# Attention and gated products on one core: down products split in two, summary scores for 128 queries at a time, a new order

## The chip, the core and the metric

The kernel runs on one core of a Trainium2 chip. The core has a matrix engine (TensorE, PE in the profile; its weight loads are a track of their own, PEld), VectorE (DVE), ScalarE (ACT), GpSimd (POOL) and SyncE (SP), which here issues all transfers. Time is the device time of one execution in microseconds (us), the median over several runs. All times of this section and the next ones are of the kernel before.

## The reference, cut to what is computed

```python
k_sum = k.reshape(B, H, nb, 32, D).max(axis=3)          # B 4, H 8, S 768, D 64, nb 24
v_sum = v.reshape(B, H, nb, 32, D).mean(axis=3)
scores_l = q @ k.T / 8, kept where |i - j| < 16, else -1e9
scores_s = q @ k_sum.T / 8 + log(32)
a = softmax(concat(scores_l, scores_s))                 # 768 + 24 columns
x = (a @ concat(v, v_sum)) as rows of 512               # 3072 tokens
h = x @ w_in                                            # 512 -> 2048
out = (h * cos(h)) @ w_out                              # 2048 -> 512
```

Each query sees the 31 keys around it and 24 block summaries of its sequence. The two large products at the end hold nearly all of the arithmetic.

## The kernel before, in words

The 3072 tokens are cut into 8 blocks of 384, two to a sequence. A block has 4 groups (a, b, c, d in the order's names), each a pair of heads. For a group the kernel lays q and k out with the head dimension on the partitions, the first head on partitions 0 to 63 and the second on 64 to 127 (`qd`, `kd`), where the last 24 columns of `kd` are the summaries of k. A group's 384 queries are six tiles of 64 (`t`); tile `t` belongs to chunk `c = t // 2` and half `s = t % 2`, and its scores stand in a bank of PSUM per head, in partitions `s * 64` and up, columns 0 to 95 for a window of 96 keys and columns 96 to 119 for the 24 summaries. `scores` (L562) issues for each tile and head one product with 96 columns and one with 24, all with a 64 by 64 block of q as weights: 24 products for a group. They are in full float32, so each becomes two pairs of a weight load and a matmul in the trace: 48. For the groups of the first two blocks the mask is added by products with a 128 by 128 identity as weights and 360 columns (L549). Then come maximum, exponent, sums, the turning of the probabilities (in the first three blocks by products with the identity, L619: 120 columns of weights) and `values` (L663: 12 products with 120 by 64 weights), which leave x split into a high and a low part (`xh`, `xl`).

The gated part runs in 128 steps (8 blocks by 16 slices of the hidden dimension). A step has `up` (L707: 12 products, 384 columns), then on ACT and DVE `turns`, `residue`, `sine`, `square`, `gate`, then `high_part` (`gh`, a rounded copy, on ACT or DVE) and `low_part` (`gl`, the rest, on POOL or DVE), then `down` (L751: for each of three chunks of 128 tokens the products gh by the high weights, gh by the low weights, gl by the high weights, 512 columns each, added in one bank per chunk). After the last step of a run `take` copies the three sums, negated, to a buffer and `store` sends them out. The 16 slices of the weights are split into high and low parts by ScalarE, VectorE and GpSimd in the first third of the span.

The order of everything is written out by hand: a long string `ORDER` of tokens (`d2.sc.3.4` is scores of group d of block 2 into banks 3 and 4, `s39.up.0` is the up products of step 39 into bank 0, a last `a`, `v` or `p` names ScalarE, VectorE or GpSimd). The tokens are issued in this order and each engine executes its own instructions in it; the SP queue too issues its transfers in it and waits in it.

Of the kernel before, what the change touches and what calls it, by code (L numbers as in the profile page):

```python
# [10 lines left out]
F32 = mybir.dt.float32  # L11
F32R = mybir.dt.float32r
# [15 lines left out]
c0.q b0.k a0.q a0.k d0.k c0.k b0.tk.0.0 v0_0.l b0.tk.1.1 b0.ck.0.a b0.ks.0 a0.tq.2 b0.ck.1.a b0.ks.1 v0_1.l a0.cq.a  # L28
a0.tk.0.3 a0.tk.1.4 a0.ck.0.a a0.ks.0 b0.q a0.ms.5.6 a0.ck.1.a a0.ks.1 d0.tk.0.7 d0.tk.1.0 w1.l d0.ck.0.a d0.ks.0
a0.sc d0.ck.1.a d0.ks.1 c0.tk.0.1 a0.z.1.a c0.tk.1.2 c0.ks.0 c0.tq.3 a0.z.0.a d0.q c0.ms.4.7 c0.ks.1 c0.ck.0.a a0.mx  # L30
c0.ck.1.a c0.cq.a v0_0.h.v a0.su w0.l c0.sc v0_1.h.v v0_0.s.p a0.ex c0.v b0.tq.0 b0.ms.6.5 v0_1.s.v b0.cq.a c0.z.1.a
b0.sc c0.z.0.a a0.sm a0.v w1.ab.0 c0.mx d0.tq.1 b0.z.0.a d0.ms.2.3 a0.iv w1.cl a0.nm b0.z.1.a d0.cq.a w1.sh.6.7 a0.m
d0.sc c0.su w1.lb a0.tp.0.0 w0.ab.1 a0.tp.1.4 d1.q w1.fb.0 a0.cp.0.a w2.l a0.cp.1.a w0.cl d0.z.1.a w1.hi.a w5.l
w0.sh.0.1 a0.va.5 d0.z.0.a b0.m w1.lo.p w0.lb c0.ex d0.m a0.xh.a d0.mx c0.sm d0.su w3.l c0.iv w2.ab.1 a0.xl c0.nm
w0.fb.0 d0.ex b0.v c0.tp.0.6 w2.cl w0.hi.a d0.sm c0.tp.1.7 c0.cp.0.a w0.lo.p c0.m w2.sh.2.3 c0.cp.1.a w2.lb w5.ab.1
c1.q w2.fb.0 a1.q d0.iv w2.hi.a w5.cl d0.nm d0.v w5.sh.4.5 c0.va.0 w4.l w5.lb w3.ab.1 w2.lo.p d1.m d0.tp.0.1 c0.xh.a
b0.mx d0.tp.1.6 c0.xl d0.cp.0.a b0.su a1.tq.7 b1.q w5.fb.0 d0.cp.1.a d0.va.2 a1.cq.a a1.m b0.ex w3.cl a1.ms.3.0
w5.hi.a w3.sh.6.7 d1.v a1.sc d0.xh.a w5.lo.p b0.sm w4.ab.1 c1.tq.1 c1.v c1.ms.4.5 w3.lb a1.z.1.a a1.z.0.a b1.tq.0
b0.iv b1.m w4.cl b0.nm c1.cq.a b1.cq.a a1.mx c1.sc c1.m w4.sh.0.1 c1.z.1.a a1.su b0.tp.0.3 c1.z.0.a b0.tp.1.5 d0.xl
a1.v b0.cp.0.a w4.lb b1.ms.4.2 b0.cp.1.a a1.ex w8.l c1.mx b0.va.3 b1.v a1.sm b1.sc c1.su b0.xh.a b0.xl d1.tq.5  # L40
b1.z.1.a a1.iv s0.up.3 a2.q w4.fb.0 a1.nm c1.ex b1.z.0.a b2.v c1.sm w4.hi.a d1.ms.2.0 c1.iv w3.fb.1 s0.tu c1.nm
d1.cq.a a1.tp.0.1 w7.l w4.lo.v s1.up.4 w3.hi.a w9.l a1.cp.0.a w3.lo.p b1.mx w8.ab.0 w6.l d1.sc s0.re s1.tu w8.cl
a1.tp.1.5 v1_0.l s2.up.6 d1.z.0.a w10.l b1.su d1.z.1.a s1.re a1.cp.1.a s0.si d1.mx a1.va.7 w8.sh.0.1 d1.su a2.tq.2
a2.v c1.tp.0.5 s0.sq w8.lb s1.si s1.sq c1.cp.0.a s0.ga s1.ga c1.tp.1.5 s0.hi.a w8.fb.1 s1.hi.a s0.lo.p c1.cp.1.a
w9.ab.0 s0.dn.3.4.5 s1.lo.p w8.hi.v b2.q s2.tu d1.ex s2.re w8.lo.p a2.cq.v a1.xh.v s3.up.0 a1.xl s2.si d1.sm v1_0.s.p
d1.iv w9.cl c1.va.1 s2.sq d1.nm v1_1.l s3.tu s1.dn c1.xh.a s3.re w7.ab.1 c1.xl s2.ga s2.hi.a w7.cl s4.up.2 s3.si
s2.lo.p w9.sh.6.7 s3.sq b1.ex v1_1.s.p s3.ga d1.tp.0.1 w9.lb d1.tp.1.0 s2.dn s4.tu b1.sm v1_2.l d1.cp.1.a d1.cp.0.a
s4.re s5.up.0 s3.hi.a b1.iv w9.fb.0 b1.nm s4.si w9.hi.v s3.lo.p d1.va.1 w7.sh.6.7 s4.sq d1.xh.a w9.lo.p s3.dn s5.tu
w7.lb w10.ab.1 s5.re s4.ga s5.si v1_2.s.p d1.xl s4.hi.a b1.tp.0.2 w7.fb.0 s5.sq b1.tp.1.1 b1.cp.0.a b1.cp.1.a s4.lo.p
s5.ga w12.l w7.hi.a b1.va.2 s5.hi.v v1_3.l s4.dn w10.cl s5.lo.p b1.xh.a b1.xl w7.lo.p w10.sh.6.7 s6.up.1 w6.ab.1  # L50
w10.lb w10.fb.0 s7.up.0 s6.tu v1_3.s.p s6.re w10.hi.a w6.cl s5.dn s7.tu s6.si w10.lo.p v1_4.l s6.sq b2.m s7.re s8.up.2
s5.ta.0.a s6.ga s5.ta.1.v s6.hi.a s5.st.0 s5.ta.2.a w6.sh.6.7 s5.st.1 s6.lo.p w12.ab.0 s5.st.2 a2.m w6.lb v1_4.s.p
s6.dn.1.3.4 s8.tu s7.si s8.re s7.sq w12.cl s8.si v1_5.l s9.up.5 s8.sq s7.ga s8.ga s7.hi.a w6.fb.1 s8.hi.a s7.lo.p
s7.dn s9.tu s8.lo.p w12.sh.6.7 w11.l w6.hi.a s9.re w6.lo.p w12.lb s9.si s10.up.0 s9.sq s9.ga w12.fb.0 s9.hi.a s8.dn
s10.tu s9.lo.p s10.re w12.hi.a w15.l v1_5.s.v w11.ab.1 w12.lo.p s11.up.2 v1_6.l s10.si w11.cl s10.sq s9.dn s11.tu
s11.re s10.ga s11.si w11.sh.6.7 s10.hi.a s12.up.5 s11.sq s10.lo.p w15.ab.0 w11.lb v1_6.s.p s10.dn s12.tu s11.ga s12.re
s11.hi.a w11.fb.1 s12.si s11.lo.p v1_7.l s13.up.0 s12.sq s12.ga w11.hi.a w13.l w15.cl s12.hi.a w15.sh.6.7 s11.dn
s13.tu s12.lo.p s13.re w11.lo.p w15.lb s13.si s12.dn s13.sq s13.ga w15.fb.0 s13.hi.a s13.lo.p s14.up.2 w13.ab.1
w15.hi.v w13.cl w15.lo.p s13.dn s14.tu v1_7.s.v s14.re a2.k s15.up.5 w13.sh.6.7 s14.si s14.sq s14.ga w13.lb s14.hi.a
s16.up.0 s15.tu s14.lo.p s15.re w13.fb.0 s15.si s14.dn s15.sq s16.tu s15.ga w14.l w13.hi.a s16.re a2.tk.0.2 s15.hi.a  # L60
w13.lo.p a2.tk.1.6 a2.ks.0 a2.ck.0.a s17.up.7 b2.k a2.ck.1.a a2.ks.1 s16.si s16.sq s15.lo.p a2.sc.5.2 s16.ga s16.hi.a
s15.dn s17.tu a2.z.1.v s16.lo.p s17.re w14.ab.1 a2.z.0.v a2.mx s17.si s16.dn s17.sq w14.cl a2.su s17.ga s17.hi.a
w14.sh.6.7 b2.tk.0.0 s18.up.2 b2.ck.0.a s17.lo.p a2.ex w14.lb s17.dn w14.fb.0 s18.tu a2.sm w14.hi.a b2.tk.1.5 s18.re
b2.tq.6 w14.lo.p b2.ck.1.a c2.k s19.up.7 b2.ks.1 s18.si b2.ks.0 c2.q b2.cq.v a2.iv b2.sc.5.0 a2.nm s18.sq s19.tu
s18.ga s20.up.6 s19.re s18.hi.a b2.z.0.v s19.si s18.lo.p b2.z.1.v s19.sq b2.mx a2.tp.0.2 s20.tu a2.tp.1.5 c2.tq.0
a2.cp.0.a s19.ga b2.su s18.dn d2.q c2.cq.v a2.cp.1.a s19.hi.a s20.re b2.ex s19.lo.p c2.tk.0.7 c2.tk.1.2 c2.ks.0 s19.dn
d2.k c2.ks.1 c2.ck.0.a b2.sm c2.ck.1.a s20.si b2.iv s21.up.5 b2.nm s20.sq s20.ga s22.up.0 s21.tu s20.hi.a s21.re
s20.lo.p s21.si s21.sq d2.tk.0.7 s20.dn s22.tu s21.ga d2.ck.0.a d2.ks.0 s21.hi.a s22.re s21.lo.p s22.si a2.va.2 s22.sq
d2.tk.1.6 s22.ga a2.xh.a c2.m s23.up.5 s22.hi.v d2.ck.1.a d2.ks.1 s22.lo.p a2.xl c2.v b2.tp.0.7 s23.tu b2.tp.1.0
c2.sc.6.2 b2.cp.0.a s23.re v2_0.l b2.cp.1.a d2.tq.7 s23.si c2.z.1.v s21.dn a3.q c2.z.0.v s23.sq d2.cq.a c2.mx s23.ga  # L70
c2.su s22.dn.0.2.6 s21.ta.1.1.a s23.hi.v s21.ta.2.0.a s21.st.1 c2.ex s21.st.2 s23.lo.p s24.up.7 c2.sm s25.up.5
s21.ta.0.1.a c2.iv c2.nm s24.tu s21.st.0 s24.re s24.si d2.sc.3.4 s23.dn d2.z.0.v d2.z.1.v s25.tu s24.sq d2.mx s26.up.1
s25.re d2.su s24.ga s25.si a3.qt s24.hi.a s25.sq b3.q s24.lo.p b2.va.3 d2.ex s25.ga s24.dn s25.hi.v b2.xh.v s25.lo.p
# [103 lines left out]
def tile_kernel(  # L177
# [25 lines left out]
    P = 128  # L203
# [491 lines left out]
    class Step:  # L695
# [76 lines left out]
        def take(self, i, *args):  # L772
            *where, eng = args
            if where:
                self.place(i, *where)
            else:
                self.o[i] = late[5][:, i * DM : (i + 1) * DM]
# [134 lines left out]
```

## Time and profile before

| what | value |
|---|---|
| median of 3 runs | 678.67 us (677.88 to 681.73) |
| the profiled execution | 679.78 us, span 678.0 us |
| mean granted TensorE clock | 0.984 |
| PE busy | 641.4 us, 95% |
| PEld busy | 564.8 us, 83% |
| DVE, ACT, POOL busy | 391.1, 411.6, 295.4 us |

The profiled execution took 1.1 us more than the median. In rows of the trace a line gives start and length in us, engine, source line, operation, output and inputs, partitions and columns of the weights (`64*64`), shape of the output and the count of instructions that the row merges. A merged row runs from the first start to the last end. The start of a matmul is recorded and its end is modelled, so rates are read from starts.

### The profile page before, as it was taken

To read this page: it belongs to the slowest core of one execution; us is meant where nothing else is said; L and a number is where in the kernel's file an instruction comes from. 1 tells how busy PE (TensorE), PEld (TensorE's weight loads), DVE (VectorE), ACT (ScalarE), POOL (GpSimd) and SP (SyncE) were. 2 spreads that over 40 slices of the span, in tenths; PEclk is the share of its full clock that TensorE was granted. 3 is DMA by queue.
4 is the path that set the end of the run, shared out by engine and by line. 5 is a ranking of instruction groups with operands and counts; after the bars stand their busy time and mean duration, and the time that the engine had idled before them with its cause. 6 is when DMAs were issued, how large, how long until landed. Compare 5 with 4: busy or idle time off the path is not lost.

```text
span 678.0 us, 13401 instructions
## 1 busy us (share of the span) xinstructions
PE 641.4 (95%) x5180; PEld 564.8 (83%) x5180; DVE 391.1 (58%) x642; ACT 411.6 (61%) x720; POOL 295.4 (44%) x312
## 2 busy tenths in 40 slices
PE   6439989999999999999999999999999999999996
PEld 4327768888888888888898888898898889899895
DVE  3889799987553467426775764248484652232221
ACT  3557887758765467646765765447666565455443
POOL 3665778655432355333444554414353442122221
PEclk9959999999999999999999999999999999999999
DMA  9797924442322323434545453433253440001001
GB/s 221 212 252 195 321 83 159 149 110 59 87 51 54 88 78 112 117 89 95 111 123 129 118 166 95 94 53 89 75 148 90 107 124 29 23 0 47 1 0 47
DMA packets 158543, 71.17 MB, mean 105 GB/s; under 512 B 129552, under 2 KB 147344, under 8 KB 158480
## 3 DMA queue, kind: packets, MB, share of 16 engines
q1 hardware_dynamic: 158480, 70.32, 39.0%
q8 instruction: 41, 0.67, 0.4%
q14 instruction: 22, 0.18, 0.1%
HBM read 52.99 MB, written 14.94 MB: 100 GB/s over the span
## 4 chain that ended last, share of the span: by engine, by line
PE 86%; DMA 5%; DVE 3%; ACT 2%; SPq 2%; POOL 2%; issue 1%; POOLq 0%; ACTq 0%; DVEq 0%
PE banks L707 38%; PE banks L751 37%; PE banks L562 4%; DMA late<-in_moe_w_out_dram 4%; PE banks L663 4%; SPq L449 1%; PE banks L549 1%; PE banks L619 1%; POOL w L349 1%; DMA kn<-in_v_dram 1%; DVE banks L400 1%; DVE banks L392 1%; DVE stage L386 1%; PE banks L495 0%; PE banks L508 0%
## 5 line engine op out<-in xcount | busy, mean ns | idle before, releaser
L707 PE MATMUL banks<-xh,w 128*128 128x384 f32 x1024 | 281.9, 338 | 0.0
L751 PE MATMUL banks<-w,gh 128*128 128x512 f32 x768 | 242.6, 397 | 0.0
L349 POOL TENSOR_TENSOR gl<-t,gh 128x384 fp32r<-128x384 f32 x123 | 126.0, 1026 | 251.1 <-ACT gh L343 185.7
L707 PEld LDWEIGHTS banks<-xh,w 128*128 128x128 f32 x1024 | 186.9, 188 | 4.7 <-DVE xl L349 0.2
L707 PE MATMUL banks<-xl,w 128*128 128x384 f32 x512 | 171.8, 336 | 0.0
L751 PEld LDWEIGHTS banks<-w,gh 128*128 128x128 f32 x768 | 140.2, 188 | 25.6 <-ACT gh L343 0.2
L751 PE MATMUL banks<-w,gl 128*128 128x512 f32 x384 | 151.7, 395 | 0.6 <-POOL gl L349 0.4
L720 DVE SCALAR_TENSOR_TENSOR t<-t,banks 128x384 f32<-128x384 int32 x128 | 70.3, 549 | 127.6 <-ACT t L717 127.4
L717 ACT ACTIVATE t<-banks 128x384 int32<-128x384 f32 x128 | 62.4, 487 | 104.0 <-PE banks L707 100.3
L732 DVE SCALAR_TENSOR_TENSOR t<-t,banks 128x384 f32<-128x384 f32 x128 | 70.2, 549 | 75.5 <-ACT t L728 75.0
L707 PEld LDWEIGHTS banks<-xl,w 128*128 128x128 f32 x512 | 96.1, 188 | 3.8
L725 ACT ACTIVATE t<-t 128x384 f32<-128x384 f32 x128 | 67.2, 525 | 44.1 <-DVE t L720 43.8
L343 ACT CAST gh<-t 128x384 fp32r<-128x384 f32 x115 | 58.8, 512 | 55.1 <-DVE t L732 50.9
L751 PEld LDWEIGHTS banks<-w,gl 128*128 128x128 f32 x384 | 72.0, 188 | 18.0 <-POOL gl L349 2.4
L728 ACT ACTIVATE t<-t 128x384 f32<-128x384 f32 x128 | 67.2, 525 | 3.6
L586 POOL TENSOR_TENSOR sc<-sc,m 128x720 f32<-128x720 f32 x28 | 40.7, 1453 | 41.8 <-DVE m L581 39.0
L610 POOL TENSOR_TENSOR sc<-sc,r 128x720 f32<-128x720 f32 x28 | 38.9, 1392 | 38.5 <-DVE r L607 33.7
L349 POOL TENSOR_TENSOR w<-stage,w 128x1024 fp32r<-128x1024 f32 x15 | 36.6, 2440 | 18.2 <-ACT w L343 17.5
L562 PEld LDWEIGHTS banks<-kd,qd 64*64 64x64 f32 x1344 | 27.5, 132 | 7.9 <-issue 5.5
L602 DVE TENSOR_REDUCE r<-sc 128x6 f32<-128x726 f32 x28 | 25.2, 902 | 14.5 <-ACT sc L599 14.4
L725 ACT ACT_TABLE_LOAD x24 | 30.8, 1283 | 0.4
L562 PE MATMUL banks<-kd,qd 64*64 64x96 f32 (+1 forms) x1344 | 30.4, 231 | 0.1
(97 smaller groups left out, 577.4 us busy)
## 6 DMA issues: line engine op xcount, KB each, us to landing
late<-in_moe_w_in_dram SPq DMA_DIRECT2D x16, 512.0 KB
late<-in_moe_w_out_dram SPq DMA_DIRECT2D x16, 512.0 KB
pd<-stage SPq DMA_DIRECT2D x20, 384.0 KB
vn<-in_v_dram SPq DMA_DIRECT2D x52, 120.0 KB
out_dram<-stage SPq DMA_DIRECT2D x24, 256.0 KB
pt<-pd SPq DMA_DIRECT2D x60, 96.0 KB
kn<-in_v_dram SPq DMA_DIRECT2D x24, 192.0 KB
qn<-in_q_dram SPq DMA_DIRECT2D x80, 48.0 KB
```

The source lines that it names most:

```text
L343: eng.copy(out=out, in_=in_)
L349: eng.tensor_tensor(out=lo, in0=src, in1=hi.bitcast(F32), op=ALU.subtract)
L562: nc.tensor.matmul(out=self.sp[hh][s * QT : (s + 1) * QT, c, lo : lo + n], lhsT=self.qd[rows, t * QT : (t + 1) * QT], rhs=self.kd[rows, ke ...
L586: nc.gpsimd.tensor_tensor(out=self.sc, in0=self.sc, in1=self.m.unsqueeze(2).broadcast_to([P, U, NK]), op=ALU.subtract)
L610: nc.gpsimd.tensor_tensor(out=self.sc, in0=self.sc, in1=self.r.unsqueeze(2).broadcast_to([P, U, NK]), op=ALU.mult)
L707: nc.tensor.matmul(out=self.h, lhsT=w_of(name, self.f)[:, c * P : (c + 1) * P], rhs=x_of(self.blk, part, c), start=n == 0, stop=n == last,)
L717: nc.scalar.activation(out=self.t.bitcast(I32), in_=self.h, func=AF.Copy, scale=1.0 / TWO_PI)
L720: nc.vector.scalar_tensor_tensor(out=self.t, in0=self.t.bitcast(I32), scalar=-TWO_PI, in1=self.h, op0=ALU.mult, op1=ALU.add)
L725: nc.scalar.activation(out=self.t, in_=self.t, func=AF.Sin, scale=0.5)
L728: nc.scalar.activation(out=self.t, in_=self.t, func=AF.Square, scale=math.sqrt(2.0))
L732: nc.vector.scalar_tensor_tensor(out=self.t, in0=self.t, scalar=-1.0, in1=self.h, op0=ALU.add, op1=ALU.mult)
L751: nc.tensor.matmul(out=self.acc[i], lhsT=g[:, i * P : (i + 1) * P], rhs=w_of(name, self.f), start=self.first and n == 0, stop=self.last an ...
```

## The change

It has four parts.

The products of `down` come in two operations. `dh` issues the six products with gh, `dl` the three with gl; in between the order may place other work. In the last step of all, `dh` leaves out the third chunk and `dl` makes up for it.

In `scores` the windows' products stay as they are (64 queries, 96 columns, four of them for a chunk: two halves by two heads), while the summaries' products are made for the 128 queries of a chunk at once: weights of 64 partitions by 128 columns, 24 columns of output over all 128 partitions. A group has 12 products of 96 columns and 6 of 24 columns, instead of 12 and 12.

The last sums of a run that don't go to one of the two stage buffers get a place of their own, in the room of an x part that is no longer needed.

`ORDER` is written anew. In it 38 rather than 13 of the 128 copies `gh` go to VectorE, and 35 rather than 5 of the rests `gl`, the others staying on ScalarE and GpSimd; some of the smaller copies of the attention part move to VectorE as well.

```diff
@@ scores
-            for t in range(U):
-                c, s = divmod(t, 2)
-                k0 = self.base + t * QT
+            for c in range(QC):
+                for s, hh in itertools.product(range(2), range(2)):
+                    rows, k0 = slice(hh * D, (hh + 1) * D), self.base + (2 * c + s) * QT
+                    nc.tensor.matmul(
+                        out=self.sp[hh][s * QT : (s + 1) * QT, c, :W],
+                        lhsT=self.qd[rows, (2 * c + s) * QT : (2 * c + s + 1) * QT], rhs=self.kd[rows, k0 : k0 + W],
+                        start=not self.masks, stop=not self.masks,
+                    )
                 for hh in range(2):
                     rows = slice(hh * D, (hh + 1) * D)
-                    for lo, n, key in ((0, W, k0), (W, NB, KW)):
-                        nc.tensor.matmul(
-                            out=self.sp[hh][s * QT : (s + 1) * QT, c, lo : lo + n],
-                            lhsT=self.qd[rows, t * QT : (t + 1) * QT], rhs=self.kd[rows, key : key + n],
-                            start=not self.masks, stop=not self.masks or (c == QC - 1 and lo == W),
-                        )
+                    nc.tensor.matmul(
+                        out=self.sp[hh][:, c, W:NK],
+                        lhsT=self.qd[rows, c * P : (c + 1) * P], rhs=self.kd[rows, KW : KW + NB],
+                        start=not self.masks, stop=not self.masks or c == QC - 1,
+                    )
@@ down
-            gh, gl = self.gh, self.gl
-            for i in range(NTT):
-                for n, (g, name) in enumerate(((gh, "wo_h"), (gh, "wo_l"), (gl, "wo_h"))):
-                    nc.tensor.matmul(
-                        out=self.acc[i], lhsT=g[:, i * P : (i + 1) * P], rhs=w_of(name, self.f),
-                        start=self.first and n == 0, stop=self.last and n == 2,
-                    )
+            self.products(self.early())
+
+        def early(self):
+            chunks = range(NTT - 1 if self.g == len(steps) - 1 else NTT)
+            return [(i, n) for i in chunks for n in range(2)]
+
+        def down_low(self):
+            early = self.early()
+            rest = [(i, n) for n in range(3) for i in range(NTT) if (i, n) not in early]
+            self.products(sorted(rest) if len(rest) > NTT else rest)
+
+        def products(self, which):
+            for i, n in which:
+                g, name = (self.gl if n == 2 else self.gh), ("wo_h", "wo_l", "wo_h")[n]
+                nc.tensor.matmul(
+                    out=self.acc[i], lhsT=g[:, i * P : (i + 1) * P], rhs=w_of(name, self.f),
+                    start=self.first and n == 0, stop=self.last and n == 2,
+                )
@@ take
-            else:
+            elif self.kind == "first":
                 self.o[i] = late[5][:, i * DM : (i + 1) * DM]
+            else:
+                t = xp.tile([P, 2, TB], F32R, name="last", tag="xh0%d" % (self.blk % 2))
+                self.o[i] = t.rearrange("p c n -> p (c n)")[:, :DM].bitcast(F32)
@@ names
-            lo="low_part", dn="down", fe="fetch", ad="add", ta="take", st="store",
+            lo="low_part", dh="down", dl="down_low", fe="fetch", ad="add", ta="take", st="store",
@@ ORDER, its last tokens
...
+s127.sq s126.dh s127.ga s126.hi.a s126.dl s127.hi.a s127.lo.v s127.dh s127.dl s127.ta.1.1.v s127.ta.0.0.a s127.ta.2.a s127.st.0
+s127.st.2 s127.st.1
```

The first place is on PE: the scores of group d of block 2 and what stands around them, before. Line L562 is `scores`, L707 `up`, L751 `down`; `kd` is the laid-out k, `qd` the laid-out q.

```order
L707 MATMUL banks<-xl_0_506,w_1017 128x384
L707 MATMUL banks<-xh_0_500,w_1017 128x384
L562 MATMUL banks<-kd_102,qd 64x96
L562 MATMUL banks<-kd_102,qd 64x24
...
L751 MATMUL banks<-w_1078,gh 128x512 x2
L751 MATMUL banks<-w_1078,gl 128x512
```

The same group in the change, where L569 is the windows' and L576 the summaries' product, L777 the down products and L721 `up`:

```order
L777 MATMUL banks<-w_1224,gl 128x512 x3
L569 MATMUL banks<-kd_102,qd 64x96 x4
L576 MATMUL banks<-kd_102,qd 128x24 x2
L569 MATMUL banks<-kd_102,qd 64x96 x4
L576 MATMUL banks<-kd_102,qd 128x24 x2
L569 MATMUL banks<-kd_102,qd 64x96 x4
L576 MATMUL banks<-kd_102,qd 128x24 x2
L721 MATMUL banks<-xh_0_434,w_982 128x384
```

Before, products of 64 rows by 96 and by 24 columns alternate 12 times; in the change four windows' products are followed by two of the wide summaries' products, three times. All 32 groups have this form.

The second place is the end of PE's program, before: the down products of the last step.

```order
L751 MATMUL banks<-w_1456,gh 128x512 x2
L751 MATMUL banks<-w_1456,gl 128x512
L751 MATMUL banks<-w_1456,gh 128x512 x2
L751 MATMUL banks<-w_1456,gl 128x512
L751 MATMUL banks<-w_1456,gh 128x512 x2
L751 MATMUL banks<-w_1456,gl 128x512
```

And in the change, the last two steps:

```order
L777 MATMUL banks<-w_1610,gh 128x512 x6
L777 MATMUL banks<-w_1610,gl 128x512 x3
L777 MATMUL banks<-w_1419,gh 128x512 x4
L777 MATMUL banks<-w_1419,gl 128x512 x2
L777 MATMUL banks<-w_1419,gh 128x512 x2
L777 MATMUL banks<-w_1419,gl 128x512
```

The first product with gl stood third in a step; now it stands seventh, and in the last step fifth.

The third place is the end of the SP queue, where the last sums leave, before:

```order
L788 DMA out_dram<-stage_6481 128x512
L788 DMA out_dram<-stage_6483 128x512
L788 DMA out_dram<-stage_6518 128x512
L788 DMA out_dram<-stage_6935 128x512
L788 DMA out_dram<-stage_6937 128x512
L788 DMA out_dram<-stage_6941 128x512
```

And in the change:

```order
L817 DMA out_dram<-stage_6274 128x512
L817 DMA out_dram<-stage_6324 128x512
L817 DMA out_dram<-stage_6272 128x512
L817 DMA out_dram<-stage_6735 128x512
L817 DMA out_dram<-last 128x512
L817 DMA out_dram<-stage_6733 128x512
```

Before, all three of the last sums leave from the two stage buffers; now the third chunk's leaves from `last`, as the second of the three, and its copies are shared by ScalarE (first and third) and VectorE (second).

More of the change, by code (lines that the diff above doesn't have):

```diff
@@ L1 @@
+import itertools
 import math
@@ L33 @@
[L33 to L67, printed above, removed]
@@ L170 @@
+s127.sq s126.dh s127.ga s127.hi.a s126.dl s127.lo.v s127.dh s127.dl s127.ta.1.1.v s127.ta.0.0.a s127.ta.2.a s127.st.0
+s127.st.2 s127.st.1
 """
```

257 lines of the change are left out of this document (149 added, 108 removed).

## The prediction

> **What bounds the kernel now.** I read the page's busy times first, then the busy times by stretch, then single stretches of PE and of its weight loads.
>
> ```profile
> PE 641.4 (95%) x5180; PEld 564.8 (83%) x5180; DVE 391.1 (58%) x642; ACT 411.6 (61%) x720; POOL 295.4 (44%) x312
> core 0: us, PE busy (x) PEld busy (x) DVE busy (x) ACT busy (x) POOL busy (x), PEclk, DMA share, GB/s
> 17.00:34.00 17.00, 7.68 (x153) 5.55 (x144) 14.04 (x15) 8.96 (x16) 10.67 (x9) 0.95 0.75 213
> 34.00:51.00 17.00, 5.91 (x51) 5.09 (x53) 14.36 (x18) 8.77 (x13) 10.52 (x7) 0.50 0.93 252
> 51.00:68.00 17.00, 17.00 (x243) 13.16 (x240) 16.31 (x20) 12.44 (x22) 10.24 (x7) 0.95 0.71 194
> 68.00:110.00 42.00, 37.66 (x312) 31.50 (x312) 35.97 (x50) 34.65 (x57) 33.43 (x33) 1.00 0.60 183
> 110.00:150.00 40.00, 40.00 (x246) 36.08 (x247) 36.50 (x47) 27.70 (x51) 25.72 (x22) 1.00 0.50 154
> 150.00:400.00 250.00, 250.00 (x2157) 222.10 (x2156) 148.49 (x269) 161.72 (x277) 106.18 (x109) 1.00 0.38 95
> 400.00:672.00 272.00, 271.89 (x1910) 242.83 (x1908) 118.69 (x216) 149.34 (x273) 92.78 (x95) 1.00 0.25 66
> 672.00:678.00 6.00, 0.28 (x2) 0.00 (x0) 0.00 (x0) 1.30 (x3) 0.00 (x0) 0.95 0.35 131
> ```
>
> From 110 to 672 us PE is busy without a gap: 562 us in which nothing but PE's own instructions sets the time. Up to 51 us it mostly waits (DVE is the busiest there and the transfers fill up to 0.93 of their engines), from 68 to 110 us it waits 4.3 us in all, and after 672 us come 6 us of last copies and stores. So the change is worth what it does to PE's own stream, and to these 4.3 and 6 us. A wait removed between 110 and 672 us is worth nothing, since there is none.
>
> **The scores, in PE's stream.** Of the 32 groups the 24 of blocks 2 to 7 have their scores in the full stretch. One of them, with the loads around it, the values of another group, and a case where the two adjoin:
>
> ```profile
> 189.48 0.19 PEld L707 LDWEIGHTS banks<-xl,w 128*128 128x128 f32 x1
> 189.66 0.19 PEld L707 LDWEIGHTS banks<-xh,w 128*128 128x128 f32 x1
> 190.09 0.98 PEld L562 LDWEIGHTS banks<-kd,qd 64*64 64x64 f32 x48 [0.25 <-issue]
> 191.11 0.30 PEld L751 LDWEIGHTS banks<-w,gh 128*128 128x128 f32 x2
> ...
> 205.06 0.19 PEld L707 LDWEIGHTS banks<-xh,w 128*128 128x128 f32 x1
> 205.49 0.78 PEld L663 LDWEIGHTS banks<-pt,vn 120*64 120x64 f32 x24 [0.25 <-ACT t L725]
> 206.34 0.30 PEld L751 LDWEIGHTS banks<-w,gh 128*128 128x128 f32 x2
> ...
> 351.11 0.98 PEld L562 LDWEIGHTS banks<-kd,qd 64*64 64x64 f32 x48 [0.25 <-issue]
> 352.12 0.78 PEld L663 LDWEIGHTS banks<-pt,vn 120*64 120x64 f32 x24
> L562 PEld LDWEIGHTS banks<-kd,qd x1104: 129/133/135, 160.5 to 547.3; 64*64 64x64 f32 x184
> L663 PEld LDWEIGHTS banks<-pt,vn x576: 132/138/138, 176.2 to 585.9; 120*64 120x64 f32 x192
> ```
>
> Two things are to be seen. First, the pace inside a block: the last of the 48 loads starts 0.133 before the row's end, at 190.94, so 48 loads take 0.85 us, 0.018 each, 0.28 for a chunk's 16; the four 64 by 64 blocks work side by side. Second, the price of changing the shape of the weights. Among 128 by 128 weights a load follows the one before by 0.18 us (189.48 to 189.66), during the running product. The first 64 by 64 load comes 0.43 after the last full one: its product started at about 189.83 and at today's pace was through at 190.00, so the load waited for the array to run empty, 0.09 us. At the end it is the same: the last load at 190.94, its product from about 191.00 to 191.02, the next load at 191.11, 0.09 later. From full width to 120 by 64 it is also 0.43 (205.06 to 205.49), back again the last load stands at 206.13 and the next at 206.34, and from 64 by 64 to 120 by 64 the step is 0.16 (351.96 to 352.12). So the array runs empty at a change of columns alone (128 by 128 to 120 by 64), of rows alone, and of both, each time these rows show one.
>
> The change makes the summaries' weights 64 by 128 between windows' weights of 64 by 64: five changes of shape inside each group, where there was none. For the size I need three more rates:
>
> ```profile
> 64.75 1.37 PE L549 MATMUL banks<-mask,ident 128*128 128x360 f32 x4
> L549 PE MATMUL banks<-mask,ident x5: 464/466/466, 59.8 to 65.7; 128*128 128x360 f32 x5
> 200.56 0.81 PE L619 MATMUL banks<-ident,sc 128*120 128x128 f32 x6
> L619 PE MATMUL banks<-ident,sc x24: 270/272/273, 163.7 to 221.6; 128*120 128x128 f32 x24
> ```
>
> A float32 matmul of 360 columns takes (1.37 - 0.466) / 3 = 0.30 us, so 96 columns 0.080 and 24 columns 0.020. Full-width loads with a short product follow each other by (0.81 - 0.272) / 5 = 0.108. The 24 loads of `values`, 64 wide in two halves of the array, take (0.78 - 0.138) / 23 * 2 = 0.056 a pair. Check on a chunk of today: two passes of 96 columns 0.160, two of 24 columns hidden behind loads of 0.056 each: 0.27, measured 0.28.
>
> A chunk of the change: first load 0.056, two passes of 96 columns 0.160, the lag of the fourth block behind the first 0.05, empty array 0.09, a 128-wide load 0.108, the second one 0.108 behind it (longer than the 0.020 product that covers it), the last product 0.020 and the second head's lag 0.013, empty array 0.09. That is 0.69 us against 0.28. Three chunks: 2.07 us, where today it is 1.02 from the first load to that of what follows (190.09 to 191.11). **Each group costs PE 1.05 us more**, and 24 of them 25.2 us. Bounds for a group: if the array did not run empty and a 64 by 128 load took no longer than a 64 by 64 one, 12 fewer loads at 0.018, -0.21; if the two heads' 128-wide loads also had to go one after the other, 6 * 0.108 more, +1.7. I take 1.05, since shape changes cost in every row above.
>
> The Trainium skill, page "TensorEngine Tiling (Array Packing)", section Tiling Modes, Key Properties, says that changing the tiling mode, and not only the tile, drains the engine, and lists 64 by 64 and 64 by 128 as two modes; the trace's drains of 0.09 agree, though no run here shows the 64 by 128 mode yet. By that sentence the sum is the 25.2 us above; without it, rival one.
>
> The eight groups of blocks 0 and 1 have the same form. Four run their scores while PE waits anyway (before 51 us), three between 51 and 62 us and one after it. These four cost 4.2 us if nothing absorbs them; the 4.3 us that PE waits from 68 to 110 us takes most of it up. I take +1.5 (0 to 4.2).
>
> **The down products in two operations.** PE waits for `gl` in these cases:
>
> ```profile
> PEld banks L751 <- POOL gl L349: 2.4, 5, 0.8
> 670.38 0.19 PEld L751 LDWEIGHTS banks<-w,gl 128*128 128x128 f32 x1 [0.53 <-POOL gl L349]
> 113.86 2.08 PE banks L751 x9
> L349 DVE TENSOR_TENSOR gl<-t,gh 128x384 fp32r<-128x384 f32 x5 | 2.9, 583 | 2.0 <-ACT gh L343 1.9
> L345 DVE CAST gh<-t 128x384 fp32r<-128x384 f32 x13 | 6.0, 461 | 1.5 <-DVE t L732 0.5
> ```
>
> In a step's 9 products of 2.08 / 9 = 0.23 us four more now stand ahead of it, 0.92, more than the longest wait of 0.8. The 0.53 at the end is gained in full; of the other 1.9, all before 110 us, other waits take up some. I take -1.4 (-0.5 to -2.4). The number of products, their columns and their loads stay: nothing else is gained in the full stretch. The copies and rests moved to VectorE (25 of 0.46 and 30 of 0.58 us, 29 us) are hidden: it works 148 of 250 us from 150 to 400.
>
> **The last sums.**
>
> ```profile
> 671.62 1.08 ACT L781 ACTIVATE stage<-banks 128x512 f32<-128x512 f32 x2 [2.44 <-PE banks L751]
> 672.25 3.12 SPq L788 DMA_DIRECT2D out_dram<-stage  x3
> 674.41 0.60 ACT L781 ACTIVATE stage<-banks 128x512 f32<-128x512 f32 x1 [1.70 <-DMA out_dram<-stage]
> ```
>
> The third copy waits 1.70 for a stage buffer to be stored. With a place of its own it starts when the last product is done, at 672.3 to 672.4, 2.0 earlier. On SP its store is followed by the second chunk's, whose issue takes some 0.36 (today's third copy ends at 675.01 and the row of issues at 675.37), so I take -1.5 (-1.0 to -2.0).
>
> **The new order** at the start: the same loads in nearly the same sequence, the same work ahead of the first `up`, which stands at 62.6 us now. I take 0, with 2 us to either side.
>
> ```profile
> 62.57 0.44 PE L707 MATMUL banks<-xh,w 128*128 128x384 f32 x1
> ```
>
> **Sum**: 25.2 + 1.5 - 1.4 - 1.5 = +23.8. On the profiled execution, 679.8 us (span 678.0), this gives 703.6; it lies 1.1 above the median shown, so against the median of 678.67 the forecast is **702.5 us**. Its own range adds the ends: scores 22.8 to 28.8 (0.95 to 1.2 a group), the four early groups, the two gains and the order: 695 to 711.
>
> **Rivals.** *One: no empty array between 64 by 64 and 64 by 128.* For it: the rows stay the same, only the span of columns changes. Against: from 128 by 128 to 120 by 64 too only columns change, and the array ran empty. Then 128-wide loads alone set the pace: a chunk is 0.080 + 0.108 + 0.108 + 0.056 = 0.35, +0.2 a group, +5 for 24; with the gains of 2.9 and half of the early cost, 678.7 + 5 + 0.5 - 2.9 = 681.3.
>
> *Two, the other side: the block becomes shorter.* If the loads are paced by their number (0.018 each), 36 instead of 48 save 0.21 a group, 5 in all; with 2.9 from the waits and the last sums the time is 678.7 - 7.9 = 670.8. For it: the 16 loads of a chunk do come at an even pace. Against: that pace is also what the sum of products and loads gives. It decides as soon as a group's scores on PE grow by less than 2.9 / 24 = 0.12 us.
>
> *Three: the change doesn't do to the time what it does to PE.* Were PE to wait elsewhere for what VectorE and GpSimd do, 1 us more a group would move nothing, and the time stays within 3 us of 678.7 less the gains. The rows from 110 to 672 us speak against it: no idle PE to fill.
>
> The Trainium skill, page "TensorE: Matmul & The Clock Gate", section LDWEIGHTS, gives a load's time by its columns alone, whatever the rows: about 0.107 us for 128 and 0.053 for 64. The trace agrees (0.108 and 0.056), though the 0.056 is of 120 rows; it speaks against rival two.
>
> **How the numbers follow.** The forecast 0.83, rival one 0.05, rival two 0.08, rival three 0.04. The forecast's range of 695 to 711 widened a little at the lower side for partly hidden changes of shape gives 692 to 712, which leaves out rivals one to three and some 3 in 100 of the forecast. Faster by over 0.5% (3.4 us, about what a measurement of this kernel can tell from no change): rival two and half of three, 0.10; within 0.5%: rival one in half and the rest of three, 0.04; slower 0.86.
>
> **What would show it.** In the changed trace a group's scores, from the first load to that of what follows, should take 2.0 to 2.1 us with five steps inside where no load starts for about 0.2 us; the last `down` has no wait for `gl`; the last copy no wait for a store; PE stays gapless from about 110 to 696 us. If the score blocks are at 1.3 or below, the price of a change of shape is wrong; if they are at 2.1 and the time is below 690, something else in PE's stream got shorter, and I have overlooked it.

## The result, and the profile after

The changed kernel takes **700.52 us** (median of 4 runs, 699.68 to 701.15). The kernel before, run beside it, takes 679.94 (4 runs, 677.88 to 681.73). The ratio is 1.0314, with a 95% interval of 1.0282 to 1.0346: 3% slower, inside the predicted range and 2.0 us under the forecast. The profiled execution took 699.68 us, 697.9 of it span.

First the page's busy times and the busy times by stretch, of the kernel after (columns as in the prediction: the stretch, its length, then busy time and count of PE, PEld, DVE, ACT and POOL, the granted clock of PE, the share of the DMA engines and GB/s):

```profile
PE 673.4 (96%) x4796; PEld 581.9 (83%) x4796; DVE 422.2 (60%) x727; ACT 377.8 (54%) x672; POOL 252.0 (36%) x261
51.00:68.00 17.00, 16.10 (x166) 12.04 (x160) 14.34 (x20) 12.20 (x23) 7.44 (x6) 1.00 0.58 149
68.00:110.00 42.00, 40.03 (x301) 34.27 (x302) 39.48 (x56) 34.22 (x57) 30.28 (x29) 1.00 0.51 158
110.00:150.00 40.00, 39.52 (x227) 34.88 (x226) 35.79 (x51) 25.50 (x46) 19.44 (x16) 1.00 0.56 169
150.00:400.00 250.00, 250.00 (x1857) 217.04 (x1856) 150.16 (x283) 136.80 (x236) 88.11 (x83) 1.00 0.35 85
400.00:692.00 292.00, 292.00 (x1920) 257.82 (x1919) 144.91 (x272) 142.81 (x268) 77.48 (x78) 1.00 0.26 69
692.00:697.90 5.90, 1.63 (x8) 1.01 (x6) 0.69 (x1) 1.20 (x2) 0.00 (x0) 0.91 0.35 133
```

PE has 384 instructions fewer and is busy 32 us longer; some 9 of the 32 lie ahead of the first `up`, where PE waits in between anyway (43.20 against 34.57 us busy up to 61 us). From 150 to 692 us it has no gap, as before; between 68 and 150 us it now stands idle 1.97 + 0.48 us, where it was 4.34. So the time was not lost to more waiting: PE's own stream got longer, while it worked.

Where it got longer is seen in the weight loads around one group's scores, after (start, length of the row, then how many loads it holds):

```profile
188.89 0.53 PEld L777 LDWEIGHTS banks<-w,gl 128*128 128x128 f32 x3
189.78 0.21 PEld L569 LDWEIGHTS banks<-kd,qd 64*64 64x64 f32 x8 [0.36 <-issue]
190.11 0.30 PEld L576 LDWEIGHTS banks<-kd,qd 64*128 64x128 f32 x4
190.44 0.21 PEld L569 LDWEIGHTS banks<-kd,qd 64*64 64x64 f32 x8
190.77 0.30 PEld L576 LDWEIGHTS banks<-kd,qd 64*128 64x128 f32 x4
191.11 0.21 PEld L569 LDWEIGHTS banks<-kd,qd 64*64 64x64 f32 x8
191.43 0.30 PEld L576 LDWEIGHTS banks<-kd,qd 64*128 64x128 f32 x4
191.77 0.19 PEld L721 LDWEIGHTS banks<-xh,w 128*128 128x128 f32 x1
```

From the first score load to the next other load it is 191.77 - 189.78 = 1.99 us, where it was 1.02; by the starts of the single loads 1.983 against 1.017 in all 24 groups of blocks 2 to 7, to within 0.001. A chunk takes 0.66, and the rows part at each change of shape: the last of a row's 64 by 64 loads starts 0.13 before the row's end, at 190.52, and the next 64 by 128 load 0.25 later. The other way it is 0.22. So each group costs PE 0.966 us more, and 24 of them 23.2 us.

The end, after (SPq is the SP queue that issues the stores; in brackets the idle time before an instruction and what released it):

```profile
690.92 0.56 DVE L358 TENSOR_TENSOR gl<-t,gh 128x384 fp32r<-128x384 f32 x1 [0.64 <-ACT gh L352]
692.34 0.61 PE L777 MATMUL banks<-w,gl 128*128 128x512 f32 x2
693.24 0.39 PE L777 MATMUL banks<-w,gl 128*128 128x512 f32 x1
693.67 0.60 ACT L810 ACTIVATE last<-banks 128x512 f32<-128x512 f32 x1 [0.31 <-PE banks L777]
694.29 0.33 SPq L817 DMA_DIRECT2D out_dram<-last  x1
694.72 0.38 SPq L817 DMA_DIRECT2D out_dram<-stage  x1
```

The rest `gl` of the last step starts at 690.92 and the first product that needs it at 692.34, behind the products with `gh`: no wait is left there. The last copy waits for its product alone (0.31), no more 1.70 for a store. From the start of the last product to the end of the span it is 697.9 - 693.24 = 4.66 us. Before, that product started at 671.88 and the span ended at 678.0: 6.1 us.

```profile
671.88 0.40 PE L751 MATMUL banks<-w,gl 128*128 128x512 f32 x1
```

The first `up` and PE's wait for the down products' input, after:

```profile
61.38 0.42 PE L721 MATMUL banks<-xh,w 128*128 128x384 f32 x1
PEld banks L777 <- ACT gh L352: 2.9, 4, 1.2
```

With these marks the span's 19.9 us more come apart: 1.2 less up to the first `up` (61.38 against 62.57), 22.6 more from there to the start of the last product (631.87 against 609.31), 1.45 less behind it. The 22.6 are 23.2 of the 24 groups, 1.0 of the one early group behind the first `up`, less 1.9 of PE's idle time between 60 and 150 us; 0.3 is left over.

### The profile page after: what moved, and what is told of

Same layout as the page of the kernel before. It is cut to its first block, busy times and chain, and to the rows that moved or that the text cites. A ratio compares the mean times of both kernels' runs of the same rounds, so it can differ in the third digit from the quotient of the medians.

```text
span 697.9 us, 12553 instructions
## 1 busy us (share of the span) xinstructions
PE 673.4 (96%) x4796; PEld 581.9 (83%) x4796; DVE 422.2 (60%) x727; ACT 377.8 (54%) x672; POOL 252.0 (36%) x261
## 4 chain that ended last, share of the span: by engine, by line
PE 90%; DVE 3%; DMA 2%; ACT 2%; SPq 2%; issue 1%; DVEq 0%; ACTq 0%
PE banks L777 38%; PE banks L721 36%; PE banks L576 5%; PE banks L569 5%; PE banks L677 4%; PE banks L558 1%; DMA late<-in_moe_w_out_dram 1%; DMA late<-in_q_dram 1%; PE banks L633 1%; SPq L458 1%; PE banks L517 1%; DMA late<-in_k_dram 1%; ACT stage L390 0%; PE banks L504 0%; SPq L495 0%
## 5 line engine op out<-in xcount | busy, mean ns | idle before, releaser
L721 PE MATMUL banks<-xh,w 128*128 128x384 f32 x1024 | 284.0, 338 | 0.5 <-ACT pt L352 0.5
L777 PE MATMUL banks<-w,gh 128*128 128x512 f32 x768 | 201.1, 397 | 1.6 <-ACT gh L352 1.5
L358 POOL TENSOR_TENSOR gl<-t,gh 128x384 fp32r<-128x384 f32 x93 | 94.4, 1016 | 287.9 <-ACT gh L352 155.4
L721 PEld LDWEIGHTS banks<-xh,w 128*128 128x128 f32 x1024 | 187.2, 188 | 5.8 <-ACT pt L352 0.7
L721 PE MATMUL banks<-xl,w 128*128 128x384 f32 x512 | 171.9, 336 | 0.0
L777 PEld LDWEIGHTS banks<-w,gh 128*128 128x128 f32 x768 | 140.6, 188 | 26.9 <-ACT gh L352 2.9
L777 PE MATMUL banks<-w,gl 128*128 128x512 f32 x384 | 111.6, 398 | 0.0
L721 PEld LDWEIGHTS banks<-xl,w 128*128 128x128 f32 x512 | 96.2, 188 | 4.4
L777 PEld LDWEIGHTS banks<-w,gl 128*128 128x128 f32 x384 | 70.3, 188 | 14.9
L352 ACT CAST gh<-t 128x384 fp32r<-128x384 f32 x90 | 45.8, 509 | 44.2 <-DVE t L746 43.2
L587 DVE SCALAR_TENSOR_TENSOR sc<-banks,mask 128x360 f32<-128x360 f32 x48 | 24.8, 523 | 27.4 <-PE banks L576 27.2
L569 PE MATMUL banks<-kd,qd 64*64 64x96 f32 x672 | 33.3, 268 | 1.9 <-ACT kd L352 1.0
L576 PE MATMUL banks<-kd,qd 64*128 64x24 f32 x336 | 34.0, 276 | 0.0
L576 PEld LDWEIGHTS banks<-kd,qd 64*128 64x128 f32 x336 | 25.3, 184 | 9.9
```

What stands on the lines that cost most here:

```text
L352: eng.copy(out=out, in_=in_)
L358: eng.tensor_tensor(out=lo, in0=src, in1=hi.bitcast(F32), op=ALU.subtract)
L569: nc.tensor.matmul(out=self.sp[hh][s * QT : (s + 1) * QT, c, :W], lhsT=self.qd[rows, (2 * c + s) * QT : (2 * c + s + 1) * QT], rhs=self.kd ...
L576: nc.tensor.matmul(out=self.sp[hh][:, c, W:NK], lhsT=self.qd[rows, c * P : (c + 1) * P], rhs=self.kd[rows, KW : KW + NB], start=not self.m ...
L721: nc.tensor.matmul(out=self.h, lhsT=w_of(name, self.f)[:, c * P : (c + 1) * P], rhs=x_of(self.blk, part, c), start=n == 0, stop=n == last,)
L777: nc.tensor.matmul(out=self.acc[i], lhsT=g[:, i * P : (i + 1) * P], rhs=w_of(name, self.f), start=self.first and n == 0, stop=self.last an ...
```

## The experiments

All kernels below compute the whole reference. Times are medians beside the kernel before on the same chip: 677.89 us (14 runs) for the first four kernels, 678.55 (29 runs) for the other four; the row "after" is that of the result, beside 679.94. The table holds what I read from each trace; "block" is the mean time from a late group's first score load to the next other load, "stream" the time from the start of the first `up` to that of the last product, "tail" from there to the end of the span.

| kernel | time us (runs) | ratio (95%) | block | first `up` | stream | tail |
|---|---|---|---|---|---|---|
| before | 677.89 and 678.55 | 1 | 1.017 | 62.57 | 609.31 | 6.11 |
| after | 700.52 (4) | 1.0314 (1.0282 to 1.0346) | 1.983 | 61.38 | 631.87 | 4.66 |
| after, old scores | 674.07 (9) | 0.9937 (0.9912 to 0.9963) | 1.017 | 60.99 | 607.86 | 4.65 |
| before, new scores | 706.23 (4) | 1.0415 (1.0380 to 1.0449) | 1.982 | 61.58 | 637.77 | 6.14 |
| one change of shape | 684.27 (4) | 1.0101 (1.0067 to 1.0134) | 1.437 | 59.69 | 620.46 | 4.65 |
| three changes of shape | 692.58 (4) | 1.0213 (1.0181 to 1.0245) | 1.710 | 60.85 | 625.20 | 4.64 |
| old scores, third sum in a stage buffer | 675.34 (10) | 0.9952 (0.9932 to 0.9971) | 1.017 | 60.97 | 607.89 | 6.57 |
| before, down products split | 678.08 (10) | 0.9991 (0.9969 to 1.0012) | 1.017 | 58.54 | 609.07 | 6.11 |
| old scores, nine products late | 677.94 (10) | 0.9998 (0.9981 to 1.0015) | 1.035 | 57.42 | 613.36 | 4.64 |
| old scores, five pairs adjoined | 673.03 (6) | 0.9918 (0.9896 to 0.9940) | 1.017 | 59.63 | 607.16 | 4.65 |

My theory was the prediction's: the scores lose some 24 us, nearly all of it by changes of shape; the other three parts gain a little. The rivals: the time goes with the new order, and not with the scores; or it goes with the width of the summaries' loads, and not with the changes of shape.

**The changed kernel with the old scores.** The order, the split and the place for the last sums stay; the old loop is put back:

```diff
-            for c in range(QC):
-
-                for s, hh in itertools.product(range(2), range(2)):
...
-                        out=self.sp[hh][:, c, W:NK],
-                        lhsT=self.qd[rows, c * P : (c + 1) * P], rhs=self.kd[rows, KW : KW + NB],
...
+            for t in range(U):
+                c, s = divmod(t, 2)
+                k0 = self.base + t * QT
                 for hh in range(2):
                     rows = slice(hh * D, (hh + 1) * D)
+                    for lo, n, key in ((0, W, k0), (W, NB, KW)):
+                        nc.tensor.matmul(
+                            out=self.sp[hh][s * QT : (s + 1) * QT, c, lo : lo + n],
+                            lhsT=self.qd[rows, t * QT : (t + 1) * QT], rhs=self.kd[rows, key : key + n],
...
```

> The changed kernel with the scores of the kernel before (12 products of 96 and 12 of 24 columns, all with 64 by 64 weights); the split down products, the place of the last sums and the new order stay. Theory (the changes of shape in the scores cost 0.97 us a group, everything else is small): 24 groups in PE's full stretch give 23.2 us back, the early groups up to 2 more: 675 to 678 us, and a scores block at 1.02 us. Rival (a good part of the loss comes from the new order or the split): above 682 us.

Measured 674.07, ratio 0.9937: with the old scores the rest of the change is 0.6% faster than before, and the block is back at its old length:

```profile
143.74 0.19 PEld L716 LDWEIGHTS banks<-xh,w 128*128 128x128 f32 x1
144.18 0.98 PEld L571 LDWEIGHTS banks<-kd,qd 64*64 64x64 f32 x48 [0.25 <-issue]
145.19 0.77 PEld L772 LDWEIGHTS banks<-w,gh 128*128 128x128 f32 x4
```

That the new order brings the loss falls with this run. From the first load of the first late group to PE's last product it takes 668.85 - 144.18 = 524.67 us, the changed kernel 693.24 - 145.48 = 547.76: 23.1 us more, and 24 times 0.966 are 23.2. So the scores, which are all that differs, account for the whole of it. The time is just under the 675 to 678 that I expected; the gain of 3.8 us (2.5 to 6.0 by the interval) can't be told from the 2.9 that I had given the waits and the last sums.

**The kernel before with the new scores alone.** The same edit the other way round.

> The kernel before with the new scores alone; its order, its down products and its last sums stay. Theory: 24 groups at 0.97 us more, and up to 4 us for the early groups: 702 to 706 us, slower than the whole change because the gains of the waits and the last sums are missing. Rival (the new order brings the loss): below 690 us.

Measured 706.23, ratio 1.0415, just above what was expected. The blocks are as long as in the changed kernel (1.982), so the 24 groups cost the same 23.2 us here. The trace shows where the rest is from, in the waits of the weight loads (total, times, longest) and in the stretches:

```profile
PEld banks L757 <- POOL gl L350: 4.9, 6, 2.3
68.00:110.00 42.00, 37.49 (x289) 31.34 (x287) 35.32 (x48) 33.39 (x55) 29.64 (x31) 1.00 0.54 169
110.00:150.00 40.00, 37.99 (x182) 33.64 (x183) 35.11 (x43) 25.19 (x44) 22.92 (x22) 0.96 0.40 128
```

The waits for `gl` double, from 2.4 to 4.9 us, and PE idles 4.51 + 2.01 from 68 to 150 us, 2.2 more than before: the down products meet a rest that isn't there yet. The group behind the first `up` costs another 1.0 us, and from 112.27 to 115.68 us the granted clock was 0.50 in this execution, which is worth up to 1.7 us. Together with the 23.2 that makes 28.1 of the stream's 28.5 us. In the changed kernel's list of waits the down products have none for `gl`. Whether the two parts simply add up the times can't tell: 4.15% for the scores alone less 0.63% for the rest make 3.5%, both together cost 3.14%, and the intervals are wider than the difference.

**One change of shape in a group, and three.** Same products, same 36 loads; only their sequence within a group differs.

```diff
-            for c in range(QC):
 
+            def windows(c):
                 for s, hh in itertools.product(range(2), range(2)):
...
+            def summaries(c, last):
                 for hh in range(2):
...
-                        start=not self.masks, stop=not self.masks or c == QC - 1,
+                        start=not self.masks, stop=not self.masks or last,
...
+            for c in range(QC):
+                windows(c)
+            for c in range(QC):
+                summaries(c, c == QC - 1)
```

For three changes the sequence is `windows(0)`, `summaries(0)`, `summaries(1)`, `windows(1)`, `windows(2)`, `summaries(2)`.

> The changed kernel, but in each group all 12 windows' products first and then all 6 summaries' products: the same products, loads and columns, with one change of shape inside a group instead of five. Theory (the empty array at a change is what costs): a block is 0.65 us of windows and 0.76 of summaries, 1.41 instead of 1.98 us, and the kernel 24 * 0.57 = 13.7 us faster than the change: 686 to 687 us. Rival (the wide weights' loads cost, wherever they stand): a block stays at 1.9 to 2.0 and the time at 700 us.

> The changed kernel with the order windows 0, summaries 0 and 1, windows 1 and 2, summaries 2 in each group: three changes of shape inside a group. Theory: a block of 0.33 + 0.55 + 0.49 + 0.33 = 1.70 us, the kernel 24 * 0.285 = 6.8 us faster than the change: 693 to 694 us, halfway between one and five changes. Rival (wide loads alone): 700 us.

Measured 684.27 and 692.58, with blocks of 1.437 and 1.710. The times lie below the 686 to 687 and 693 to 694 that I expected; I had counted from the 700.5 us of the result, and the kernel before ran 2 us faster beside these runs. The weight loads, first with one change:

```profile
145.37 0.54 PEld L569 LDWEIGHTS banks<-kd,qd 64*64 64x64 f32 x24 [0.25 <-issue]
146.03 0.75 PEld L578 LDWEIGHTS banks<-kd,qd 64*128 64x128 f32 x12
146.81 1.23 PEld L784 LDWEIGHTS banks<-w,gh 128*128 128x128 f32 x6
```

and with three:

```profile
144.75 0.21 PEld L569 LDWEIGHTS banks<-kd,qd 64*64 64x64 f32 x8 [0.25 <-issue]
145.07 0.52 PEld L578 LDWEIGHTS banks<-kd,qd 64*128 64x128 f32 x8
145.63 0.37 PEld L569 LDWEIGHTS banks<-kd,qd 64*64 64x64 f32 x16
146.12 0.30 PEld L578 LDWEIGHTS banks<-kd,qd 64*128 64x128 f32 x4
146.46 1.22 PEld L786 LDWEIGHTS banks<-w,gh 128*128 128x128 f32 x6
```

Per group, with 0, 1, 3 and 5 changes of shape: 1.017, 1.437, 1.710, 1.983. From 1 to 3 it is 0.273 and from 3 to 5 again 0.273: **0.137 us for each change**. The step from 0 to 1 less one change, 1.437 - 1.017 - 0.137 = 0.28, is what is left for all else that the wide summaries bring: wider loads, 12 fewer of them, and products of 24 columns that no longer hide behind the windows' loads. So of the 0.966 of a group 5 * 0.137 = 0.68 are changes of shape and 0.28 is this rest, which no run divides further. That the width alone sets it falls: then all three sequences would take the same time. That the change of columns alone between 64 by 64 and 64 by 128 costs nothing (the prediction's rival one) falls too. The row of 12 wide loads also shows that the two heads' loads go side by side: six pairs in 0.56 us from the first load to the last (0.75 less the 0.19 of one load), 0.11 a pair; one after the other they would take twice that. Even the cheapest of the three sequences with wide summaries stays 1% slower than before.

One thing changes together with the shape of the weights in all these runs: the windows' products write 64 partitions of a bank and the summaries' products all 128 of the same bank. That the price belongs to the weights and not to this was not tested here; the last experiment finds a price too where the two neighbours write to different banks.

**The third last sum in a stage buffer again**, all else as in the changed kernel with the old scores:

```diff
-s127.dl s127.ta.1.1.v s127.ta.0.0.a s127.ta.2.a s127.st.0
+s127.dl s127.ta.1.1.v s127.ta.0.0.a s127.ta.2.0.a s127.st.0
```

> The changed kernel with the old scores, but the third of the last sums goes to a stage buffer again. Theory: its copy waits for the store of the first sum, so from the last matmul to the end it takes 1.5 us longer than with a place of its own (6.1 instead of 4.7 us), and nothing before it moves: 675 to 676.5 us. Rival (the place makes no difference): the end stays at 4.7 us.

Measured 675.34. Its stream is that of the kernel it was made from (607.89 against 607.86), and the tail is 6.57 against 4.65:

```profile
669.00 3.56 SPq L812 DMA_DIRECT2D out_dram<-stage  x3
671.13 0.60 ACT L805 ACTIVATE stage<-banks 128x512 f32<-128x512 f32 x1 [2.16 <-DMA out_dram<-stage]
```

The copy waits 2.16 us for the store of the buffer's last content. The place of its own is worth 1.9 us in the trace. The two ratios differ by 0.0015, which is 1.0 us, and their intervals overlap.

**The split alone**, in the old order: each `dn` of the order becomes `dh dl`, one right after the other, so that the products with `gl` stand behind all with `gh`.

```diff
-s98.dn d7.mx s100.tu
+s98.dh s98.dl d7.mx s100.tu
```

> The kernel before with the split alone: in its old order each down product is followed at once by its second half, six products with gh and then three with gl, and the last step as in the change. Theory: only the waits for gl go, 0.5 us at the end and up to 1.9 us before 110 us: 676 to 678 us beside 678, with no wait for gl left in the last step. Rival (the split itself makes PE faster or slower in the full stretch): more than 3 us away from the kernel before.

Measured 678.08, ratio 0.9991 (0.9969 to 1.0012): between 2.1 us faster and 0.8 slower, so the runs can tell it neither from nothing nor from the 1.4 that I had forecast for this part. The waits for `gl` do go, from 2.4 us to 0.2, but in their place stands another, at the products with `gh`:

```profile
PEld banks L809 <- ACT gh L389: 1.0, 1, 1.0
PEld banks L709 <- DVE gl L395: 0.2, 1, 0.2
68.00:110.00 42.00, 38.42 (x266) 33.20 (x266) 37.75 (x51) 34.47 (x58) 31.49 (x34) 0.96 0.56 179
```

PE idles 3.58 us in this stretch instead of 4.34, and the clock granted in it was 0.96 instead of 1.00: 3.41 us of it, from 73.39 on, ran at 0.50, with `up` products 0.32 us apart instead of 0.175. That takes back some 1.7 us, and more than the idle time gained. The stream is 0.24 us shorter.

**All nine products late.** Made from the changed kernel with the old scores: the new order stays, but `dh` issues nothing and all nine products stand at the place of `dl`.

```diff
             self.acc = list(accs)
-            self.products(self.early())
...
         def down_low(self):
-            early = self.early()
-            rest = [(i, n) for n in range(3) for i in range(NTT) if (i, n) not in early]
-            self.products(sorted(rest) if len(rest) > NTT else rest)
+            self.products([(i, n) for i in range(NTT) for n in range(3)])
```

> The changed kernel with the old scores and all nine down products of a step together at the place of the second half, so that the new order is kept without the split. Theory: PE's full stretch has no waits that the split could remove, so only the last step's wait for gl comes back: within 1 us of the same kernel with the split (674 to 675). Rival (the new order needs the split): 3 us or more slower.

This missed. Measured 677.94, ratio 0.9998: 3.9 us slower than the kernel it was made from, and as fast as before. Its stream is 5.5 longer, though the first `up` came early:

```profile
PEld banks L765 <- POOL gl L358: 2.4, 6, 0.8
PEld banks L672 <- ACT gh L352: 1.3, 1, 1.3
PEld banks L765 <- DVE gl L358: 1.1, 2, 0.6
150.00:400.00 250.00, 248.56 (x2141) 219.78 (x2140) 156.62 (x298) 144.08 (x250) 87.97 (x85) 1.00 0.38 96
```

The waits for `gl` are back, and for the first time PE idles in the stretch behind 150 us, 1.44 us (and 0.23 more from 400 to 660). With the idle time from 60 to 150 us, 4.66 against 2.41, that makes 3.9 of the 5.5. Another 0.43 lies inside two of the 24 late score blocks, which take 1.218 and 1.246 us instead of 1.017 (at 235.03 and 333.24; why is open). Two products with `gl`, at 442.19 and 548.96, start 0.56 us late in all, and only 0.23 of that counts as idle, since the modelled end of the product before reaches into the wait. About 0.8 I could not place. So this order needs the split: without it the products with `gl` come before their rest is there. For the split alone and for the order without it (and this kernel even has the place for the last sums) no gain can be measured; both together, even without that place, make the kernel faster (0.9952, 0.9932 to 0.9971, two experiments above). I had expected the place of the products to be indifferent here, since PE has nothing to wait for behind 110 us; that holds for the old order, and for the new one only with the split.

**Fewer changes of shape between groups.** If a change of shape has a price wherever it stands, it is also paid at the edges of the score blocks. Five times the scores of one group and the values of another are put next to each other in the order of the changed kernel with the old scores; each pair has three changes of shape instead of four.

```diff
-c3.sc.2.5 s37.si a3.pi s38.tu
...
-b3.ex s37.hi.v d3.qt s37.lo.p
+b3.ex s37.hi.v c3.sc.2.5 a3.va.3 d3.qt s37.lo.p
```

> The changed kernel with the old scores, and five times a group's scores and another group's values are moved next to each other on PE, where full-width products stood between them (group a of block 3 with d of 2, a5 with c4, b5 with d4, d4 with b4, c3 with a3). Theory (each change of shape costs PE time wherever it stands): five changes fewer, some 0.2 to 0.3 us each, 1 to 1.5 us: 672.5 to 673 us, the fastest of all. Rival (only changes inside a group cost): 674.

Measured 673.03, ratio 0.9918. The stream is 0.70 us shorter than in the kernel it was made from, but that takes in the opening, where the orders are the same and PE idled 0.26 us more before 110 us. Behind it the comparison is clean: from the first load of the first late group to the last product it takes 666.79 - 143.14 = 523.65 us instead of 524.67. That is 1.0 us, **0.2 for each of the five changes saved**, at the lower end of the 1 to 1.5 that I had expected, and more than the 0.137 of a change inside a group. One pair:

```profile
219.41 0.98 PEld L609 LDWEIGHTS banks<-kd,qd 64*64 64x64 f32 x48 [0.35 <-issue]
220.43 0.78 PEld L710 LDWEIGHTS banks<-pt,vn 120*64 120x64 f32 x24
221.28 1.22 PEld L810 LDWEIGHTS banks<-w,gh 128*128 128x128 f32 x6
```

It has the lowest median of all, 0.8% below the kernel before. Against the kernel it was made from the time can't decide (the intervals of the two ratios overlap); that the five pairs help by 1.0 us rests on one trace of each. The kernel with the third sum in a stage buffer, whose products are those of the kernel this one was made from, repeats their time from 142 us on within 0.001 us, so the 1.0 is well clear of what this stretch varies by. Each pair trades two changes to or from full width for one between 64 by 64 and 120 by 64; that this saves 0.2 and not 0.137 says that the price isn't the same for every change.

## Why the prediction was right, step by step

**The scores** (+25.2 for the late groups) were the right mechanism, and 2.0 us too dear. All late groups grew by 0.966 instead of 1.05. The failing figure is the lag of the fourth block behind the first, which I put at 0.05 a chunk: from the first 64 by 64 load to the first 64 by 128 load it is 190.77 - 190.44 = 0.33, where 0.056 + 0.160 + 0.05 + 0.09 gave 0.356. So the lag is about 0.02, and that is also how far the starts of the first four loads of a chunk lie apart (190.445 to 190.465). The other half of a chunk, 0.339 by the sum, measured 0.335 (190.771 to 191.106). The empty array at a change of columns alone, which rival one denied, is there at each change (0.25 us from load to load on the way to 64 by 128, 0.22 back). The Trainium skill, page "TensorEngine Tiling (Array Packing)", section Tiling Modes, Key Properties, says that a change of the tiling mode drains the engine; the runs agree, with 0.137 us for a change between 64 by 64 and 64 by 128.

**The early groups** (+1.5) can't be told apart. The one behind the first `up` costs 0.97; the others stand ahead of it, and the first `up` came 1.2 earlier and not later. But the same opening has a first `up` that differs by more than that from one execution to another (below).

**The down products in two operations** (-1.4): what I saw of the waits was right, since they went from 2.4 to 0.2 us with the split alone, and the 0.53 at the end is gone. That their end is the whole story was wrong: the sum has no term for the products with `gh`, which now come first and wait for `gh`. In the changed kernel this wait is 2.9 us, the largest of the down products, where it was 0.2. What counts there is PE's idle time between 60 and 150 us, 1.9 less, which the split and the order make together; alone, the split is worth no gain that can be measured.

**The last sums** (-1.5): measured -1.45 by the tail, and 1.9 where the place alone was undone.

**The new order** (0, with 2 either side): the start came 1.2 us earlier in the profiled execution. The old-scores run gives the order, the split and the place together -3.8 us in time, where I had -2.9; undoing the place gives back 1.9 in the trace and about 1 in the ratio (0.9952 against 0.9937), so order and split have some 2 to 3 of it between them, and for neither without the other can a gain be measured.

In sum, 23.2 + 1.0 - 1.9 - 1.45 - 1.2 = 19.6 of the span's 19.9. The prediction's sum was 23.8, so for these two executions it was 3.9 too high: 2.0 by the lag, 1.2 by the start, 0.5 each by the early groups and by the waits of the down products, less the 0.3 left over. By the medians the change costs 20.6, so the sum was 3.2 too high there. That the forecast lies only 2.0 us above the measured median is partly luck: I had added the sum to 678.67 us, and beside the change the kernel before took 679.94, which hides 1.3 of the 3.2. Rival two, a shorter block paced by the number of loads, falls: with 36 loads instead of 48 the block grew in every sequence. Rival three falls: what each group cost PE came out in the time. Two small slips in the working: the terms of a chunk add to 0.695 and three chunks to 2.085 instead of 2.07, and by its own row (271.89 of 272.00) PE is idle for 0.11 us in the stretch up to 672, at the last step's wait for `gl`.

The signs named ahead came true but for two details: the block is 1.98 and not 2.0 to 2.1, and PE is gapless only from about 150 us to 692, with 0.48 us idle between 110 and 150.

## What to carry to other kernels

When PE has no gap, count its changes of weight shape before its instructions: here a group with 12 loads fewer takes 0.97 us more, because five changes of shape at 0.137 came in, and 0.28 with the wider loads. Sort products so that one shape runs as long as it can, and let blocks of narrow weights adjoin (0.2 us a pair here). Two parts of a change may need each other: try each alone, and the rest without it, before giving the gain to one of them.

## What I had not expected

Inside a group the price of a change of shape doesn't depend on how long the runs of equal shape around it are: from one to three changes and from three to five the block grew by 0.273 us each time. Where two changes to or from full width became one between narrower shapes, it was 0.2.

The start varies: with the same order up to the first `up`, it began at 60.99 and 60.97 us in two of the kernels with the new order and the old scores, and at 57.42 in the one with the late products; with the old order at 62.57 and 58.54. Up to there PE mostly waits and the DMA engines are the busiest part (0.87 of their time up to 51 us before, 0.95 after). Differences of 1 or 2 us between two single executions say nothing, therefore, where the stream behind the first `up` still does: it repeats within 0.03 us in the two kernels that are alike up to the tail (607.86 and 607.89).

The granted clock fell to 0.96 in single stretches (68 to 110 us in the split alone, 110 to 150 in the new scores alone) where it was 1.00 in the others, which adds up to 1.7 us to a stream that is otherwise alike. In both it is one piece of 3.41 us at 0.50, and all changes of the granted clock in these traces lie a multiple of 3.41 us apart. With the time cut into such pieces, PE was busy for only 1.58 and 1.57 us of the piece just before. Between 60 us and the last products these are the only two pieces of all ten traces with PE busy for less than half; the next, with 0.54 and 0.56, were followed by the full clock. Here, it seems, a wait of PE was paid twice: once as a wait, and once in the clock behind it. That is two cases and not a rule: in the opening of the kernel with three changes of shape a piece with PE busy for 0.73 of it (from 50.8 us) was followed by one at 0.50 too, and no run was made to test it.
